# Block sums of the output matrix kept in float32 through DRAM, their additions queued behind the splits, and the last third of the last group by plain products

## The chip, the core and the metric

The kernel runs on one core of one Trainium2 chip. The time is the device time of one execution in microseconds (us). Before the change it is 1063.64 us, the median of 3 runs that lie between 1061.75 and 1066.62. TensorE multiplies matrices, VectorE, ScalarE and GpSimd (POOL in the profile) work on tiles in on-chip memory, and SyncE (SP) issues most transfers. "Granted clock" is TensorE's clock as a share of 2.4 GHz.

## The reference, cut to what matters

```
x   = attention(q, k, v, bias(w1, b1, w2))      # 2304 tokens x 512
x   = moe1(x)                                   # 2304 x 512
gate = 1 / (1 + exp(-(x @ w_gate)))             # 2304 x 1536
val  = x @ w_val                                # 2304 x 1536
out  = (gate * val) @ w_out                     # 2304 x 512, float32
```

Everything is float32. The change touches only the last three lines, the second MLP.

## The kernel before, in words

**Numbers.** TensorE multiplies float16. Each float32 matrix is therefore scaled and kept as two float16 halves, a high one (a rounded copy) and a low one (what the rounding left), and one float32 product becomes three float16 products: high by high, high by low, low by high. `w2h16[0]`, `[1]` and `[2]` are the split matrices w_gate, w_val and w_out, each as 12 row blocks of 128 by 512; `w2f[2]` is w_out still in float32, in the same memory.

**Groups.** The 2304 tokens are 18 tiles of 128, in five groups of 4, 2, 4, 4 and 4 tiles. Groups 0 and 1 are computed by plain products: `gate_val` makes one of 12 blocks of the 1536 hidden columns at a time (24 matmuls on TensorE, L1446; a sigmoid on ScalarE, L1451; the product of the two on VectorE, L1452; and the split into halves `gv`, L1315 on ScalarE and L1316 on VectorE), `second_out` multiplies by w_out (L1649). Groups 2 to 4 replace the eight products of a two-by-two block multiplication by seven, at the price of sums of blocks made beforehand: sums of weight blocks (`w2_sums`), of input blocks (`x2_sums`, `next_sums`), and of the blocks of w_out. `gate7` makes one third (`jc` 0, 1, 2) of a group's hidden columns that way (products L1410, additions on VectorE L1334 and on POOL L1225, the split of the results into pieces `ap`), and `out7` multiplies that third by w_out (L1557), adding into four result tiles `c`. The last third of the last group has its own `out_last`, which ends in the output.

**The block sums of w_out before the change.** For each `jc` four sums of four blocks are needed. `out_adds` makes them in float32 on POOL, three tiles at a time, as soon as the third of w_out is decoded. After all 12 splits of w_out, `out_split` scales each sum (ScalarE, L1249), rounds it (ScalarE, L1250), takes the low half (POOL), and stores both halves to a scratch tensor `to_d` in DRAM. Behind the plain groups `out_sums` loads the halves back: three of the four sums into a tile of their own (`w3s`), the fourth over the block b12 of `w2h16[2]`, which no later product of groups 2 to 4 reads.

**What sets the order.** The decoding of w_out, its additions, its scale, its splits (`w2_split`: the scaled copy `w2tmp` on POOL, L722, or on ScalarE, L720; the high half on ScalarE, L723; the low half on POOL, L724) and the sums' splits form a list of units, which `take` deals out between the gate blocks of group 0: 5 cost units before each of the first 8 blocks, then 7. Within an engine instructions run in the order of the code, except where `issue_after` queues something behind a named instruction: the sums of weights and of group 2's input (`fs`, `w2s`, `x2s`) stand on VectorE behind the low half of the tenth gate block, `glob["so"]`. `next_sums(3, ...)` makes the input sums of group 3, half of them per call, behind the last VectorE instruction of `gate7(0)` of group 2. Working tiles (`fr`, `c`, the eight product tiles `prod`) are rings: an instruction that writes one waits until the last reader of its previous content is done.

Of the kernel before, what the change touches and what calls it, by code (L numbers as in the profile page):

```python
# [102 lines left out]
def attn_moe_kernel(  # L103
# [20 lines left out]
    to_d = dram.tile([3, 128, 4, 2, 2, 256], F16, name="to_d")  # L124
# [1104 lines left out]
    def out_adds(jc):  # L1229
        if jc == 0:  # L1230
            four = [sw_p.tile([128, 3, 2, 256], F32, name=f"w2s{m}{n}") for n in (1, 2) for m in range(2)]
            tmps.update((n, four[n // 3][:, n % 3]) for n in range(12))
# [3 lines left out]
        padd(u, b12, b11, ALU.subtract)  # L1236
        padd(x, b22, u, ALU.subtract)
        padd(y, b22, b12, ALU.subtract)
        padd(v, b21, x, ALU.subtract)

    def behind_splits(jc):
        with tc.issue_after(glob["split"].ins):
            out_split(jc)

    def out_split(jc):
        for n in range(4):
            f = tmps[4 * jc + n]
            d = xs_p.tile([128, 2, 2, 256], F16, name=f"x2s{n}")
            act.activation(out=f, in_=f, func=ACTF.Copy, scale=sw[:, jc, S_O:S_O + 1])  # L1249
            act.activation(out=d[:, 0], in_=f, func=ACTF.Copy)  # L1250
            padd(d[:, 1], f, d[:, 0], ALU.subtract)
            sp.dma_start(out=to_d[jc, :, n], in_=d)
# [10 lines left out]
    units += [(1, lambda jc=jc: behind_splits(jc)) for jc in range(3)]  # L1263
# [21 lines left out]
    xb = {}  # L1285
# [4 lines left out]
    def load_x2(g):  # L1290
        n, o = sizes[g], first[g]
        t = ring("xb", [128, 4, 4, 2, 128], F16)
# [8 lines left out]
    grow("fr", 2, ctx, "left")  # L1301
# [208 lines left out]
    def out_sums(jc):  # L1510
        b11, b21, b12, b22 = out_blocks(jc)
        st_ = w3_p.tile([128, 3, 2, 2, 256], F16, name=f"w3s{jc}")
        sp.dma_start(out=st_, in_=to_d[jc, :, 1:4])
        for l in range(2):
            sp.dma_start(out=b12(l), in_=to_d[jc, :, 0, l])

        def part(n):
            return lambda l, kk=None: st_[:, n, l] if kk is None else st_[:, n, l, kk]
        osum[jc] = dict(b11=b11, b21=b21, b22=b22, t1=b12, t2=part(0), t3=part(1), t4=part(2))
# [9 lines left out]
    def gate7(jc, xs_):  # L1529
# [50 lines left out]
    def out_last(g, jc, ps):  # L1580
        w = osum[jc]
        a, b, c = (f32t() for _ in range(3))
        c11, c12, c21, c22 = cs[g]

        def done_(c_, p, th, e, halves=((0, 2),)):
            act.activation(out=c_, in_=c_, func=ACTF.Copy, scale=col(CO))
            for lo, hi in halves:
                dve.scalar_tensor_tensor(out=c_[:, lo:hi], in0=p[:, lo:hi], scalar=col(CO), in1=c_[:, lo:hi],
                                         op0=ALU.mult, op1=ALU.add)
                put(g, th, e, c_, range(lo, hi), (sp, act))  # L1590

        act.activation(out=a, in_=oproduct(ps["a", 1, 1], w["b11"]), func=ACTF.Copy)
        add(b, oproduct(ps["s", 2], w["t2"]), a)
        add(c11, c11, a)
        add(c, oproduct(ps["s", 3], w["t3"]), b)
        add(c22, c22, c)
        p2 = oproduct(ps["a", 1, 2], w["b21"])
        done_(c11, p2, 0, 0)
        add(c21, c21, c)
        add(c12, c12, b)  # L1600
        p5 = oproduct(ps["s", 1], w["t1"])
        add(c12, p5, c12)
        done_(c22, p5, 1, 1)
        p4 = oproduct(ps["a", 2, 2], w["t4"])
        done_(c21, p4, 1, 0)
        p3 = oproduct(ps["s", 4], w["b22"])
        done_(c12, p3, 0, 1, ((0, 1), (1, 2)))
# [84 lines left out]
    grow("fr", 6, ctx, "left")  # L1692
# [91 lines left out]
```

## Time and profile before

| | |
|---|---|
| median of 3 runs | 1063.64 us (1061.75 to 1066.62) |
| profiled execution | 1058.2 us, its span 1056.4 us |
| TensorE busy | 890.7 us, 84% |
| VectorE busy | 819.7 us, 78% |
| ScalarE busy | 681.5 us, 65% |
| POOL busy | 573.7 us, 54% |

The shares are means over stages with different limits; the stage in question runs from about 640 us to the end. A timeline row gives a start, a length, an engine, a line of the kernel, the operation, out<-in and a count; in brackets stands the idle time of the engine ahead of it and what ended that.

### The profile page before, as it was taken

To read this page: it belongs to the slowest core of one execution; us is meant where nothing else is said; L and a number is where in the kernel's file an instruction comes from. 1 tells how busy PE (TensorE), PEld (TensorE's weight loads), DVE (VectorE), ACT (ScalarE), POOL (GpSimd) and SP (SyncE) were. 2 spreads that over 40 slices of the span, in tenths; PEclk is the share of its full clock that TensorE was granted. 3 is DMA by queue.
4 is the path that set the end of the run, shared out by engine and by line. 5 is a ranking of instruction groups with operands and counts; after the bars stand their busy time and mean duration, and the time that the engine had idled before them with its cause. 6 is when DMAs were issued, how large, how long until landed. Compare 5 with 4: busy or idle time off the path is not lost. (4 is left out here: it accounts for less than half of the span.)

```text
span 1056.4 us, 25115 instructions
## 1 busy us (share of the span) xinstructions
PE 890.7 (84%) x9944; PEld 664.0 (63%) x9944; DVE 819.7 (78%) x1546; ACT 681.5 (65%) x1352; POOL 573.7 (54%) x506
## 2 busy tenths in 40 slices
PE   2646665778878899999989788887899989999997
PEld 2624444555656666776766464344478878888886
DVE  6879899876767757676758977579975997877888
ACT  4788886768877888888868986774342433443432
POOL 3357656657566665566543579347001446787355
PEclk9776576689999999999999999998989999999999
DMA  7978999899999999999678344012103131013001
GB/s 225 298 229 221 244 248 242 228 208 216 188 195 194 180 207 180 182 208 218 132 188 310 130 141 150 1 40 100 71 20 131 41 110 41 1 61 103 9 2 41
DMA packets 266838, 156.71 MB, mean 148 GB/s; under 512 B 217312, under 2 KB 239840, under 8 KB 266720
## 3 DMA queue, kind: packets, MB, share of 16 engines
q1 hardware_dynamic: 262848, 151.44, 58.9%
q0 software_dynamic: 2048, 1.58, 0.6%
q10 hardware_dynamic: 1824, 2.09, 0.5%
q8 instruction: 78, 1.28, 0.5%
q14 instruction: 40, 0.33, 0.1%
HBM read 87.17 MB, written 25.43 MB: 107 GB/s over the span
## 5 line engine op out<-in xcount | busy, mean ns | idle before, releaser
L618 POOL TENSOR_TENSOR p<-p,p 128x1024 f16<-128x1024 f32 x72 | 159.1, 2209 | 122.4 <-ACT p L617 80.7
L1225 POOL TENSOR_TENSOR ap<-fr,ap 128x512 f16<-128x512 f32 x45 | 59.1, 1327 | 141.7 <-ACT ap L1525 137.1
L606 ACT ACTIVATE p<-p,m,sc 128x576 f32<-128x576 f32 x144 | 123.9, 862 | 2.4
L1334 DVE TENSOR_TENSOR fr<-prod,fr 128x512 f32<-128x512 f32 x144 | 96.1, 686 | 35.9 <-PE prod L1410 16.3
L1446 PE MATMUL s_ps<-xb,w2f 128*128 128x512 f16 (+1 forms) x576 | 105.5, 345 | 21.8 <-DVE fr L1452 20.6
L599 DVE CUSTOM_DVE_ANT_0 p<-score,gk 128x576 f32<-128x576 f32 x144 | 103.0, 751 | 12.2 <-PE score L581 7.8
L848 PE MATMUL x2ps<-lt,w1f 128*128 128x128 f16 x1728 | 105.0, 220 | 3.2 <-ACT lt L836 2.0
L848 PEld LDWEIGHTS <-w1f 128*128 128x128 f16 x1728 | 100.2, 99 | 3.5 <-issue 1.1
L1446 PEld LDWEIGHTS <-w2f 128*128 128x128 f16 x576 | 59.2, 103 | 68.2 <-issue 28.9
L642 PE MATMUL xps<-gk,pt 128*128 128x64 f16 (+1 forms) x2240 | 87.3, 202 | 14.5 <-DMA pt<-p 12.5
L642 PEld LDWEIGHTS <-pt 128*128 128x128 f16 (+1 forms) x2240 | 82.0, 107 | 24.2 <-DMA pt<-p 14.7
L1410 PEld LDWEIGHTS <-w2f 128*128 128x128 f16 x864 | 84.5, 98 | 14.2 <-issue 4.3
L465 PEld LDWEIGHTS <-mask 128*128 128x128 f16 (+1 forms) x1312 | 59.6, 115 | 52.4 <-issue 23.8
L1525 ACT ACTIVATE ap<-fr 128x512 f16<-128x512 f32 x63 | 38.8, 628 | 79.9 <-DVE fr L1536 44.0
L1557 PEld LDWEIGHTS <-ap 128*128 128x128 f16 x756 | 73.8, 98 | 10.1 <-DVE c L1334 1.5
L791 PE MATMUL hps<-w1f,xt 128*128 128x512 f16 x312 | 75.8, 389 | 5.0 <-DVE gk L264 2.3
L576 PE MATMUL score<-gk,qt 64*128 64x512 f16 x384 | 61.2, 426 | 14.4 <-DVE m L599 6.3
L465 PE MATMUL bp<-rhs,mask 128*128 128x64 f16 (+1 forms) x960 | 47.9, 216 | 27.5 <-DVE gb L491 10.6
L1410 PEld LDWEIGHTS <-w2s 128*128 128x128 f16 x648 | 63.4, 98 | 8.7 <-issue 1.4
L791 PEld LDWEIGHTS <-xt 128*128 128x128 f16 x384 | 37.5, 101 | 47.1 <-issue 11.8
L617 ACT ACTIVATE p<-p 128x1152 f16<-128x1152 f32 x54 | 62.4, 1157 | 6.1 <-DMA pt<-p 4.1
L604 ACT ACTIVATE m<-m,sc 128x1 f32<-128x1 f32 x144 | 39.3, 286 | 36.2 <-DVE m L599 35.9
(236 smaller groups left out, 2164.8 us busy)
## 6 DMA issues: line engine op xcount, KB each, us to landing
gk<-bias_d SPq DMA_DIRECT2D x24, 576.0 KB
wraw<-in_moe_w_out_dram SPq DMA_DIRECT2D x20, 512.0 KB
sraw<-in_q_dram SPq DMA_DIRECT2D x12, 384.0 KB
sraw<-in_k_dram SPq DMA_DIRECT2D x12, 384.0 KB
sraw<-in_v_dram SPq DMA_DIRECT2D x12, 384.0 KB
bias_d<-gk SPq DMA_DIRECT2D x8, 576.0 KB
qraw<-in_q_dram SPq DMA_DIRECT2D x64, 64.0 KB
kv<-in_k_dram SPq DMA_DIRECT2D x32, 128.0 KB
```

The source lines that it names most:

```text
L465: pe.matmul(big[0:np_, jj // 8, o:o + 64], lhsT, rhs[i].rearrange("p c h g -> p (c h g)"), start=(i == 0), stop=(i == 1),)
L599: dve.tensor_tensor_reduce(out=pp[:, hh], in0=score[:, 960 * hh:960 * hh + S], in1=bi, scale=1.0, scalar=-3.0e38, op0=ALU.add, op1=ALU.max ...
L606: act.activation(out=pp[:, hh], in_=pp[:, hh], func=ACTF.Exp, bias=m[:, 2 + hh:3 + hh], scale=col(C), accum_out=sm[:, c + hh:c + hh + 1])
L617: act.activation(out=hi, in_=pp, func=ACTF.Copy)
L618: pool.tensor_tensor(out=p16[:, :, 640:1152], in0=view(pp, 0, [[640, 2], [1, 512]]), in1=view(p16, 0, [[1280, 2], [1, 512]]), op=ALU.subtract)
L642: pe.matmul(o, a, b_, start=(n == 0), stop=(n == len(seq) - 1))
L791: pe.matmul(h, xt[:, xl, kk, off:off + 128], win16[:, 2 * kk + n, wl], start=(kk == 0 and xl == 0 and wl == 0), stop=(kk == 3 and xl == 1),)
L848: pe.matmul(ps[:, dc], wout16[:, f, wl, 128 * dc:128 * dc + 128], lt[:, ll, f], start=(n == 0), stop=(n == 23))
L1334: glob["dve"] = dve.tensor_tensor(out=out_, in0=a, in1=b, op=op)
L1410: pe.matmul(p[:, jf, 0:nn], w(wl, kk, jf), x(xl, kk), start=(m == 0), stop=(m == 5))
L1446: pe.matmul(ps[:, 0:n], w[:, 4 * (j // 4) + c, wl, o:o + 128], xx[:, 0:n, c, xl, :], start=(m == 0), stop=(m == 11))
L1557: pe.matmul(p[:, tt], a[:, al, kk, 128 * tt:128 * tt + 128], w(wl, kk), start=(m == 0), stop=(m == 5))
```

## The change: what it does

1. `out_adds` no longer stands where w_out is decoded: its twelve additions and stores are queued behind the last split, for `jc` 0 and 1 on POOL, for `jc` 2 on VectorE (`dadd`). The float32 sums go to `to_d` as they are. `out_split` is gone.
2. `out_sums` loads each float32 sum into one of the four `c` tiles (float32, unused until then), scales and rounds it on ScalarE and takes the low half on VectorE. There are twelve such loads, of 256 KB each.
3. Before it is overwritten, block b12 of the last third is saved to DRAM (`b12_d`), and it is loaded back behind group 3. The last third of the last group then multiplies by the plain blocks: `gate7` returns only the four gate pieces, and `out_last` makes four result blocks of 24 products each.
4. The first half of `next_sums(3, ...)` stands ahead of group 2's products. The `fr` ring has three tiles instead of two up to the plain groups' end, five instead of six behind it; the input tile of a group is as long as the group.

```diff
-    to_d = dram.tile([3, 128, 4, 2, 2, 256], F16, name="to_d")
+    to_d = dram.tile([3, 128, 4, 2, 256], F32, name="to_d")
+    b12_d = dram.tile([128, 2, 2, 256], F16, name="b12_d")
...
     def out_adds(jc):
+        with tc.issue_after(glob["split"].ins):
+            out_adds_(jc, padd if jc < 2 else dadd)
+
+    def dadd(out_, a, b, op=ALU.add):
+        dve.tensor_tensor(out=out_, in0=a, in1=b, op=op)
...
-        padd(u, b12, b11, ALU.subtract)
...
-            act.activation(out=f, in_=f, func=ACTF.Copy, scale=sw[:, jc, S_O:S_O + 1])
-            act.activation(out=d[:, 0], in_=f, func=ACTF.Copy)
-            padd(d[:, 1], f, d[:, 0], ALU.subtract)
-            sp.dma_start(out=to_d[jc, :, n], in_=d)
+        plus(u, b12, b11, ALU.subtract)
...
+        for n, f in enumerate((u, x, y, v)):
+            sp.dma_start(out=to_d[jc, :, n], in_=f)
...
-    units += [(1, lambda jc=jc: behind_splits(jc)) for jc in range(3)]
+    units += [(1, lambda: sp.dma_start(out=b12_d, in_=w2h16[2][:, 8:10, :, 256:512]))]
...
-    grow("fr", 2, ctx, "left")
+    grow("fr", 3, ctx, "left")
...
-        sp.dma_start(out=st_, in_=to_d[jc, :, 1:4])
-        for l in range(2):
-            sp.dma_start(out=b12(l), in_=to_d[jc, :, 0, l])
...
+        s_ = sw[:, jc, S_O:S_O + 1]
+        for n in (1, 2, 3, 0):
+            f, d = ctile(n), part(n - 1) if n else b12
+            sp.dma_start(out=f, in_=to_d[jc, :, n])
+            act.activation(out=d(0), in_=f, func=ACTF.Copy, scale=s_)
+            dve.scalar_tensor_tensor(out=d(1), in0=f, scalar=s_, in1=d(0), op0=ALU.mult, op1=ALU.subtract)
...
-            if (fh, th) != (0, 1):
+            if plain_ or (fh, th) != (0, 1):
                 ps["a", th + 1, fh + 1] = piece(y, padd)
+        if plain_:
+            return ps
...
-    grow("fr", 6, ctx, "left")
+    grow("fr", 5, ctx, "left")
...
+    next_sums(3, 0, add)
     for g in range(2, 5):
         p0 = gate7(0, xs_)
         if g == 2:
             with tc.issue_after(glob["dve"].ins):
-                for t in range(2):
-                    next_sums(3, t, add)
+                next_sums(3, 1, add)
...
-        p2 = gate7(2, xs_)
+        p2 = gate7(2, xs_, g == 4)
...
+        if g == 3:
+            sp.dma_start(out=w2h16[2][:, 8:10, :, 256:512], in_=b12_d)
```

`out_last` now reads, per result block, `p += a[th, kh] @ blk[kh, e]` over both `kh`, both row blocks and the three pairs of halves, and one scaled addition on VectorE per block (two for the last) before the store.

How the order on the engines moves, in three places. **First place:** ScalarE right behind the scale of w_out, before (`w2s` are the block sums, `x2s` their halves, `gv` a gate block's high half, `fr<-s_ps` a sigmoid, L720 and L723 the split of w_out):

```order
L1451 ACTIVATE fr<-s_ps,sw 128x512
L1315 ACTIVATE gv<-fr 128x512
L1451 ACTIVATE fr<-s_ps,sw 128x512
L720 ACTIVATE w2tmp<-w2f_9698,sw 128x512 x2
L1249 ACTIVATE w2s_10750<-w2s_10750,sw 128x512 x3
L1249 ACTIVATE w2s_10751<-w2s_10751,sw 128x512 x3
L1249 ACTIVATE w2s_10752<-w2s_10752,sw 128x512 x3
L1249 ACTIVATE w2s_10753<-w2s_10753,sw 128x512 x3
L723 ACTIVATE w2f_9698<-w2tmp 128x512 x2
L1250 ACTIVATE x2s_11022<-w2s_10750 128x512
```

and in the changed kernel:

```order
L1448 ACTIVATE fr<-s_ps,sw 128x512
L1312 ACTIVATE gv<-fr 128x512
L721 ACTIVATE w2tmp<-w2f_9699,sw 128x512 x2
L724 ACTIVATE w2f_9699<-w2tmp 128x512 x2
L1448 ACTIVATE fr<-s_ps,sw 128x512
L721 ACTIVATE w2tmp<-w2f_9699,sw 128x512 x2
L724 ACTIVATE w2f_9699<-w2tmp 128x512
L1312 ACTIVATE gv<-fr 128x512
L724 ACTIVATE w2f_9699<-w2tmp 128x512
```

The twelve scalings and the copies into `x2s` are no longer in the queue; gate copies and sigmoids follow the splits directly.

**Second place:** ScalarE at the third and fourth gate block (counted from 0: sigmoids two and three), before (`x2ps` is the end of the first MLP, `wraw` and `w2f` the decoding of w_out, L1178 the sum of squares for its scale):

```order
L193 ACTIVATE w2f_9698<-wraw 128x1024
L194 ACTIVATE wraw<-wraw 128x1024
L723 ACTIVATE w2f_9696<-w2tmp 128x512
L723 ACTIVATE w2f_9697<-w2tmp 128x512
L853 ACTIVATE x_10687<-x2ps 128x4x128
L1451 ACTIVATE fr<-s_ps,sw 128x512
L193 ACTIVATE w2f_9698<-wraw 128x1024
L194 ACTIVATE wraw<-wraw 128x1024
L856 DMA x_d<-x_10687 128x1024
L723 ACTIVATE w2f_9697<-w2tmp 128x512
L1451 ACTIVATE fr<-s_ps,sw 128x512
```

and in the changed kernel, where the lines stand one to three further:

```order
L724 ACTIVATE w2f_9698<-w2tmp 128x512 x2
L1179 ACTIVATE w2junk,w2st<-w2f_9699 128x1024
L194 ACTIVATE w2f_9699<-wraw 128x1024
L195 ACTIVATE wraw<-wraw 128x1024
L724 ACTIVATE w2f_9698<-w2tmp 128x512
L1179 ACTIVATE w2junk,w2st<-w2f_9699 128x1024
L854 ACTIVATE x_10688<-x2ps 128x4x128
L1448 ACTIVATE fr<-s_ps,sw 128x512 x2
L194 ACTIVATE w2f_9699<-wraw 128x1024
L195 ACTIVATE wraw<-wraw 128x1024
```

Both sigmoids now stand together, behind two sums of squares, a further decoding pair and the copy of `x`; before, one stood ahead of a decoding pair and the other behind it.

**Third place:** SP's queue where the sums are loaded back, before (`out_dram<-ob` are output stores of group 1, `xx<-x_d` loads of group 3's input):

```order
L1658 DMA out_dram<-ob 128x512 x3
L1515 DMA w2f_9698<-to_d 128x2x256 x4
L1513 DMA w3s_12099<-to_d 128x3072
L1513 DMA w3s_12103<-to_d 128x3072
L1513 DMA w3s_12107<-to_d 128x3072
L1461 DMA xx<-x_d 128x1024 x2
L1515 DMA w2f_9698<-to_d 128x2x256 x2
L1662 DMA out_dram<-ob 64x512 x2
L1658 DMA out_dram<-ob 128x512
L1471 DMA xt_d<-xx 128x2048
```

and in the changed kernel:

```order
L1516 DMA c_12066<-to_d 128x512
L1516 DMA c_12083<-to_d 128x512
L1458 DMA xx<-x_d 128x1024 x2
L1516 DMA c_12071<-to_d 128x512
L1516 DMA c_12075<-to_d 128x512
L1516 DMA c_12079<-to_d 128x512
L1516 DMA c_12100<-to_d 128x512
L1516 DMA c_12088<-to_d 128x512
L1516 DMA c_12092<-to_d 128x512
L1659 DMA out_dram<-ob 64x512 x2
L1655 DMA out_dram<-ob 128x512
L1516 DMA c_12096<-to_d 128x512
```

Seven of the twelve loads now stand behind the first pair of group 3's input loads, the last of them behind three output stores too; before, only two halves for b12 did.

## Rows read from the trace of the kernel before

**Rows 1.** Page: busy tenths in 40 slices of 26.4 us

```profile
PE   2646665778878899999989788887899989999997
...
DVE  6879899876767757676758977579975997877888
```

**Rows 2.** Stretches: window, length, busy (instructions) of PE, PEld, DVE, ACT, POOL, clock, DMA

```profile
690.80:718.40 27.60, 23.34 (x136) 12.99 (x134) 26.18 (x30) 19.77 (x35) 13.67 (x11) 1.00 0.11 39
718.40:742.10 23.70, 18.34 (x98) 10.31 (x96) 23.70 (x24) 9.27 (x20) 18.43 (x12) 0.86 0.35 134
742.10:780.00 37.90, 34.82 (x211) 21.83 (x210) 37.87 (x68) 14.65 (x28) 0.00 (x0) 0.91 0.13 42
867.00:1031.10 164.10, 163.12 (x1494) 145.73 (x1492) 131.93 (x170) 62.69 (x106) 104.85 (x92) 1.00 0.11 39
```

**Rows 3.** Waits of PE, 636 to 1057 us: total us, times, longest us

```profile
PE s_ps L1446 <- DVE fr L1452: 20.6, 7, 5.4
PE prod L1410 <- DVE fr L1334: 3.9, 2, 2.7
```

**Rows 4.** Timeline of POOL, PE and ACT, 645 to 666 us: start, length first

```profile
645.56 4.73 POOL L1225 TENSOR_TENSOR w2s<-w2f 128x512 f32<-128x512 f32 x3
...
645.84 5.35 PE L1446 MATMUL s_ps<-xb,w2f 128*128 128x512 f16 x24 [0.62 <-DVE fr L1452]
...
651.96 0.63 ACT L723 ACTIVATE w2f<-w2tmp 128x512 f16<-128x512 f32 x1 [4.32 <-POOL w2tmp L722]
...
653.58 1.12 ACT L193 ACTIVATE w2f<-wraw 128x1024 f32<-128x1024 f32 x1
...
655.02 7.03 PE L1446 MATMUL s_ps<-xb,w2f 128*128 128x512 f16 x24 [3.83 <-DVE fr L1452]
...
665.53 10.43 PE L1446 MATMUL s_ps<-xb,w2f 128*128 128x512 f16 x40 [3.48 <-DVE fr L1452]
```

**Rows 5.** Timeline of ACT and DVE, 678 to 692 us

```profile
679.67 7.44 ACT L1249 ACTIVATE w2s<-w2s,sw 128x512 f32<-128x512 f32 x12
...
690.78 0.69 DVE L1316 TENSOR_TENSOR gv<-fr,gv 128x512 f16<-128x512 f32 x1 [11.51 <-ACT gv L1315]
```

**Rows 6.** Groups of DVE by form, 718.4 to 742.1 us: busy us, mean ns

```profile
L1334 DVE TENSOR_TENSOR fs<-xb 128x512 f32<-128x512 f16 x4 | 6.4, 1639 | 0.0
...
L1334 DVE TENSOR_TENSOR fs<-fs,xb 128x512 f32<-128x512 f32 x1 | 0.7, 679 | 0.0
```

**Rows 7.** Groups of DVE by form, 745.5 to 780 us

```profile
L1334 DVE TENSOR_TENSOR fs<-w2f 128x512 f32<-128x512 f16 x13 | 8.5, 688 | 0.0
...
L1316 DVE TENSOR_TENSOR gv<-fr,gv 128x256 f16<-128x256 f32 x4 | 1.7, 425 | 0.0
```

**Rows 8.** Timeline of PE, 725 to 783 us: gate blocks of group 1

```profile
725.87 4.93 PE L1446 MATMUL s_ps<-xb,w2f 128*128 128x256 f16 x24 [5.36 <-DVE fr L1452]
...
765.46 8.22 PE L1446 MATMUL s_ps<-xb,w2f 128*128 128x256 f16 x48 [3.08 <-DVE fr L1452]
...
776.75 5.40 PE L1446 MATMUL s_ps<-xb,w2f 128*128 128x256 f16 x48
```

**Rows 9.** Groups of PE by form, 688 to 796 us: last the idle time before

```profile
L1446 PE MATMUL s_ps<-xb,w2f 128*128 128x256 f16 x288 | 37.7, 296 | 12.7 <-DVE fr L1452 12.7
```

**Rows 10.** Timeline of PE and DVE at group 2's first product

```profile
796.30 1.47 PE L1410 MATMUL prod<-xb,w2f 128*128 128x256 f16 x12 [1.14 <-ACT ob L1653]
...
799.19 0.69 DVE L1334 TENSOR_TENSOR fr<-prod,fr 128x512 f32<-128x512 f32 x1 [7.70 <-PE prod L1410]
```

**Rows 11.** Timeline of SP and DVE, 836 to 843 us

```profile
836.56 0.80 SPq L1461 DMA_DIRECT2D xx<-x_d  x2
...
840.08 2.04 DVE L1334 TENSOR_TENSOR ts<-xx 128x256 f32<-128x256 f16 x3
```

**Rows 12.** Timeline of PE and DVE at the end

```profile
1048.12 1.47 PE L1557 MATMUL prod<-w2f,ap 128*128 128x256 f16 x12
...
1050.98 2.18 DVE L1588 SCALAR_TENSOR_TENSOR c<-prod,sc,c 128x512 f32<-128x512 f32 x4
```

More of the change, by code (lines that the diff above doesn't have):

```diff
@@ L1229, in out_adds, with out_adds_ @@
     def out_adds(jc):
+        with tc.issue_after(glob["split"].ins):
+            out_adds_(jc, padd if jc < 2 else dadd)
+    def dadd(out_, a, b, op=ALU.add):
+        dve.tensor_tensor(out=out_, in0=a, in1=b, op=op)
+    def out_adds_(jc, plus):
         if jc == 0:
@@ L1235, in out_adds @@
         u, x, y, v = (tmps[4 * jc + n] for n in range(4))
-        padd(u, b12, b11, ALU.subtract)
[L1237 to L1248, printed above, removed]
-            act.activation(out=f, in_=f, func=ACTF.Copy, scale=sw[:, jc, S_O:S_O + 1])
-            act.activation(out=d[:, 0], in_=f, func=ACTF.Copy)
-            padd(d[:, 1], f, d[:, 0], ALU.subtract)
-            sp.dma_start(out=to_d[jc, :, n], in_=d)
+        plus(u, b12, b11, ALU.subtract)
+        plus(x, b22, u, ALU.subtract)
+        plus(y, b22, b12, ALU.subtract)
+        plus(v, b21, x, ALU.subtract)
+        for n, f in enumerate((u, x, y, v)):
+            sp.dma_start(out=to_d[jc, :, n], in_=f)
     steps = [(m, jc) for jc in range(3) for m in range(2)]
@@ L1291, in load_x2 @@
         n, o = sizes[g], first[g]
-        t = ring("xb", [128, 4, 4, 2, 128], F16)
+        t = ring("xb", [128, n, 4, 2, 128], F16)
         sp.dma_start(out=t[:, 0:n], in_=x2_d[o:o + n].rearrange("t p c l q -> p t c l q"))
@@ L1527, in piece, with gate7 @@
         return p
-    def gate7(jc, xs_):
+    def gate7(jc, xs_, plain_=False):
         gates, ps = {}, {}
@@ L1580, in out_last @@
     def out_last(g, jc, ps):
[L1581 to L1585, printed above, removed]
+        blk = dict(zip(((0, 0), (1, 0), (0, 1), (1, 1)), out_blocks(jc)))
+        for c_ in cs[g]:
             act.activation(out=c_, in_=c_, func=ACTF.Copy, scale=col(CO))
[L1587 to L1607, printed above, removed]
+        for n, (th, e) in enumerate(((0, 0), (0, 1), (1, 1), (1, 0))):
+            c_ = cs[g][2 * th + e]
+            p = ps_b.tile([128, 2, 256], F32, name="prod", tag="prod")
+            for tt in range(2):
+                m = 0
+                for kh in range(2):
+                    a = ps["a", th + 1, kh + 1]
+                    for kk in range(2):
+                        for (al, wl) in ((0, 0), (0, 1), (1, 0)):
+                            pe.matmul(p[:, tt], a[:, al, kk, 128 * tt:128 * tt + 128], blk[kh, e](wl, kk),
+                                      start=(m == 0), stop=(m == 11))
+                            m += 1
+                if n == 3:
+                    dve.scalar_tensor_tensor(out=c_[:, tt], in0=p[:, tt], scalar=col(CO), in1=c_[:, tt],
+                                             op0=ALU.mult, op1=ALU.add)
+                    put(g, th, e, c_, (tt,), (sp, act))
+            if n < 3:
+                dve.scalar_tensor_tensor(out=c_, in0=p, scalar=col(CO), in1=c_, op0=ALU.mult, op1=ALU.add)
+                put(g, th, e, c_, range(2), (sp, act))
     def out7(g, jc, ps):
```

## The prediction

> **What bounds the kernel now.** I read the slices of the page first [rows 1]: in the two slices from 713 to 766 us VectorE stands at 9 while TensorE is at 7 and 8, and from about 770 us on TensorE is at 9 in all slices but two. Then the table of stretches [rows 2]: from 690.8 to 780 VectorE is busy 87.8 of 89.2 us and TensorE 76.5; from 867 to 1031 it is the other way round (TensorE 163.1 of 164.1). So the first stretch ends when VectorE is through its sums, the second when TensorE is through its products, and time taken off VectorE in the second buys nothing. The waits of TensorE say the same [rows 3]: 20.6 us in seven waits for VectorE's L1452, the second step of the gate, which stands in VectorE's queue among the sums; then only 3.9 us in two waits for L1334, both near 850 us.
>
> **Part 1: additions queued behind the splits (640 to 702 us).** Before, the first three of the twelve additions (POOL, 4.73 us) stand between two scalings of the splits; ScalarE waits 4.32 us for such a scaling, the sigmoid of the fourth gate block stands right behind it, at 652.6, and TensorE starts its sixth block only at 655.02 after 3.83 us of waiting [rows 4]. That wait's cause goes, and four of the twelve additions move to VectorE. But the order of the changed kernel also puts two sigmoids behind a scaled pair, two copies and a sum of squares that stood elsewhere (the second place shown in the change). Worked through with the durations of rows 4: POOL's scaling can come at about 645.6 instead of 650.3 (where the three additions end), so ScalarE's copy behind it ends near 647.5; then one more copy (0.63), a square and a decoding pair (each 1024 columns, 1.12 an instruction), a copy, a square and a copy of x2 (0.63, 1.12 and 0.6, the last by the copy's length) stand ahead, with about 1 us of waiting for POOL between them, so the third block is emptied near 655 instead of about 644 (8 us before the fourth's 652.6) and TensorE's fifth block starts near 656 instead of 645.84. Against that, the next wait (3.48 us, at 665.5) goes. I then get TensorE through its twelfth block near 699.5 instead of 702.5, with six products of the second matrix done instead of eighteen, which is 2.6 us of work at 0.22 each (5.35 us for 24 in rows 4): the two cancel. I take 0, bounds 6 us better (all waits of this stretch go, 20.6 - 12.7 = 7.9 by rows 3 and 9) and 6 us worse (the late emptying is not caught up).
>
> **Part 2: the splits of the block sums leave the stage (679 to 796 us).** Removed from ScalarE: twelve scalings (7.44 us) and twelve copies; VectorE waits 11.51 us for a gate copy behind the scalings and the first four copies [rows 5]. Removed from POOL: twelve low halves, 18.4 us of its time in 718.4 to 742.1 [rows 2]. VectorE pays for them: beside POOL a 512-column addition takes 1639 ns, and the last of that view, which already runs beside an idle POOL, 679 [rows 6]; later, with POOL idle, 688 and for 256 columns 425 [rows 7]. The stretch holds 24 instructions [rows 2]; their forms in that view (eleven, of which rows 6 has the first and the last) sum to 26.6 us, as two of them reach over its ends; at the durations of rows 7 (19 of 0.69, 5 of 0.42) they are 15.2. So VectorE gets some 11 us back there.
> The Trainium skill speaks against counting this (Perfetto Trace Analysis, Optimizing Scalar/DVE Operations): since VectorE and POOL share a read port, moving work between the two might not help. By that rule of the Trainium skill the 11 us would be spent again, because the twelve low halves return as VectorE instructions, and the part would be worth nothing more than the earlier start.
> By the rows the twelve low halves return on VectorE at 12 x 0.69 = 8.3 us, but only four of them (2.8 us) stand ahead of the last gate of the stage; the other eight, and fourteen instructions of the next group's sums, stand between the last gate and the first product, where VectorE waited 7.7 us for TensorE [rows 10].
> The sums can also start earlier: they stand behind the tenth block's gate in both kernels, which by part 1 is emptied near 692 instead of 695.9. Together VectorE gains 4 + 11 - 3 = 12 us up to its last gate. What TensorE can gain: its waits in 688 to 796, 12.7 us [rows 9], and what runs at the lower clock after a wait (granted 0.86 and 0.91 of 2.4 GHz over the stretches from 718 and from 742 [rows 2], so for part of them at 1.2): 24 products in 4.93 us at 725.87 and 48 in 8.22 at 765.46, where 48 take 5.40 at full clock [rows 8], so 2.2 + 2.8 = 5.0. That is 17.7 us. From 699.5, TensorE's remaining work (210 products of 0.22 and 288 of 0.1125, which is 5.40 by 48: 78.6 us) would end at 778 without any wait; before it ended at 795.2. Bounds: 18 if VectorE is never late; 8 if it is late at two of the four places, and the load of the third group's input, which now stands behind thirteen stores in SP's queue, holds the sums up by up to 3 us. VectorE's 12 us are enough for all but the last few waits: I take **-15**.
>
> **Part 3: the sums come back as float32 (around the first product).** Twelve loads of 256 KB pass through four tiles, so three rounds; each round is an issue (0.4), the landing, a scaled copy on ScalarE (0.63) and a subtraction (0.69). The nearest row for the landing: two such loads are issued at 836.56 and VectorE reads them at 840.08, 3.5 us at most [rows 11]. A round is thus at most 5 us. The first is early (its loads stand behind the fourth output store, 20 us ahead of need). The second starts behind the subtractions next to the last gate, some 8 us ahead of the first product, the third 3 us later than the second ends; its last load stands in SP's queue behind three output stores that wait for the last output copy. That gives the last subtraction at 6 us after the first product's start. VectorE's first addition on a product stands behind eleven of the twelve, so it comes at about 5 us instead of 2.9 [rows 10] (799.19, the first product at 796.30). Products have eight tiles of 12 products, 12 x 0.11 = 1.3 us each, so TensorE runs 10.5 us before it must wait: cost 0. Bounds: 0 to +4, the latter if a landing takes 5 us.
> The next group's sums for one of its two tiles now stand ahead of the first product, so half of the 28 instructions that crowd VectorE around 840 leave, and with them most of the 3.9 us of waits [rows 3]: **-2.5**, bounds 0 and -3.9. The reload of the b12 block behind group 3 has 70 us until it is read: 0.
>
> **Part 4: the last third by plain products.** 96 products instead of 84: 12 x 0.11 = +1.3 us on TensorE, which runs here without a wait. Removed: seven blocks' additions, so behind the last product only one addition of half a block is left. Before, the last product ends at 1049.59 and VectorE at 1053.16 [rows 12], 3.6 us; four pieces took 2.18, so one and its wait are about 0.7. Together 1.3 - 2.9 = **-1.6**, bounds 0 and -2.5.
>
> **Sum.** 0 - 15 + 0 - 2.5 - 1.6 = -19.1. The profiled execution took 1058.2 us, so 1039.1 by its own time. It stood 5.4 us below the median of the runs shown (1063.64); at that median the sum gives **1044.5**. Bounds of the terms added: -30 and +12.
>
> **Rivals.**
> Partial: the late sigmoids of part 1 cost their 6 us and are not caught up, and VectorE is late at half of its places (-8 in part 2): 6 - 8 - 2.5 - 1.6 = -6.1, 1057.5. For it: the order does put the sigmoids there, and VectorE was the bound. Against: TensorE waited in that stretch already [rows 4].
> VectorE and POOL come out even: the 11 us are no gain, because what comes back to VectorE (twelve subtractions and four additions, 16 x 0.69 = 11 us) is paid ahead of the gates. The earlier start (-4) and the tail (-1.6) stay: -5.6, 1058.0. For it: every instruction that leaves POOL does reappear. Against: eight of the twelve stand behind the last gate. It is also what the rule quoted in part 2 from the Trainium skill (Perfetto Trace Analysis) would make of the change.
> The four tiles hold up the products (the slower side): the queues of VectorE and ScalarE are in order, and the subtractions stand ahead of the additions that empty product tiles. It decides from the point at which the last subtraction comes later than 10.5 us after the first product's start. If a round takes 22 us instead of 5 (SP held behind a store that waits for ScalarE, and ScalarE at a copy that waits for a load), the last subtraction comes at -8 + 44 = 36 us, and TensorE loses 25.5 us against the gain of 19.1: +6.4, 1070. For it: SP's queue does hold these loads behind such stores. Against: rows 11, at 3.5 us.
>
> **Chances.** The forecast (part 2 between 10 and 18 us) 0.62; partial 0.14; even 0.14; four tiles 0.10. A measurement here tells about 0.5%, 5.3 us, from no change, so faster means below 1058.3. The forecast lies there as a whole; partial and even are centred just below that bound, so 0.16 of their 0.28 count as faster and 0.12 as the same; of four tiles 0.07 count as slower and 0.03 as the same. Faster 0.78, same 0.15, slower 0.07. The range that leaves out 2 in 10 goes from 1034 (parts 1 and 2 some 5 us each better than taken) to 1060, across the two middle rivals.
>
> **What would show it.** Part 1: no addition between POOL's scalings; the fifth gate block's start on TensorE, 656 by me. Part 2: no ScalarE work on block sums behind the scale; additions on input and weight sums at 0.69, not 1.64, after POOL's twelve splits; TensorE's waits for the gate below 5 us in all after the twelfth block; first product near 781. Part 3: VectorE's first addition on a product 5 us behind it; the waits near 850 below 1.5 us. Part 4: the last addition within 1 us of the last product. The forecast is wrong if the first product starts later than 790, or if TensorE waits among the first twenty products.

## The result and the profile after

| | changed | before | ratio, 95% interval |
|---|---|---|---|
| first comparison | 1049.45 us (1047.28 to 1050.26, 4 runs) | 1063.16 us | 0.9863 [0.9835, 0.9891] |
| second comparison (after_again) | 1044.98 us (1043.19 to 1048.64, 6 runs) | 1065.65 us | 0.9818 [0.9789, 0.9846] |

The changed kernel is faster: 1049.45 us against a forecast of 1044.5, inside the range. In the first comparison 13.7 of the forecast 19.1 us came, in the second 20.7. The traces say why two comparisons of one kernel differ: the time up to the last transposition of attention's output, where every engine runs the same instructions in the same order in both kernels, is not the same from run to run. That transposition (L691 before, L692 after) and the first product of group 2 stand on TensorE at, before, in two executions (the shown one and before_again):

```profile
551.82 0.66 PE L691 MATMUL xtp<-id_sb,xn 128*128 128x128 f32 x4 [3.19 <-DVE xn L678]
```

```profile
561.39 0.66 PE L691 MATMUL xtp<-id_sb,xn 128*128 128x128 f32 x4 [3.26 <-DVE xn L678]
...
803.95 1.47 PE L1410 MATMUL prod<-xb,w2f 128*128 128x256 f16 x12 [1.14 <-ACT ob L1653]
```

and after, in the first comparison and in after_again:

```profile
562.00 0.66 PE L692 MATMUL xtp<-id_sb,xn 128*128 128x128 f32 x4 [3.24 <-DVE xn L679]
...
793.02 1.47 PE L1407 MATMUL prod<-xb,w2f 128*128 128x256 f16 x12 [2.34 <-ACT ob L1650]
```

```profile
555.02 0.66 PE L692 MATMUL xtp<-id_sb,xn 128*128 128x128 f32 x4 [3.07 <-DVE xn L679]
...
785.54 2.67 PE L1407 MATMUL prod<-xb,w2f 128*128 128x256 f16 x12 [2.64 <-DMA c<-to_d]
788.01 1.98 PE L1407 MATMUL prod<-x2s,w2s 128*128 128x256 f16 x12
```

So I read every trace from that point, P (the start of the transposition). From P to the first product, and from there to the end of the span:

| kernel | P at | P to first product | first product to end | P to end |
|---|---|---|---|---|
| before, 3 executions | 551.8, 561.4, 560.3 | 244.5, 242.6, 243.1 | 260.1, 260.1, 260.1 | 504.6, 502.6, 503.1 |
| changed, 2 executions | 562.0, 555.0 | 231.0, 230.5 | 255.5, 257.2 | 486.5, 487.7 |

Means: 503.4 to 487.1, or 16.3 us; 12.6 of them ahead of the first product (forecast 15), 3.8 behind it (forecast 4.1). The forecast, set from P of the shown execution, was 229.2 us to the first product (781 less 551.8). Behind the first product the two executions of the changed kernel differ by TensorE's clock: in after_again, after a wait of 2.64 us, the first two products took 2.67 and 1.98 us instead of 1.47 each, 1.7 us more (granted clock 0.61 from 785.54 to 789.90 us, for most of it the lower level of 1.2 GHz); in the first comparison, after 2.34 us, it was 1.00.

What was read before has these answers. TensorE's waits from the fifth gate block to the end (us in total, times, longest), beside [rows 3]:

```profile
PE s_ps L1443 <- DVE fr L1449: 10.7, 1, 10.7
PE prod L1407 <- ACT ob L1650: 2.3, 1, 2.3
PE prod L1407 <- ACT fr L1612: 1.1, 1, 1.1
PE prod L1595 <- DVE c L1599: 0.6, 1, 0.6
PE prod L1407 <- DVE c L1331: 0.2, 1, 0.2
```

Seven waits for the gate have become one, at the fifth block, and none is left behind it. TensorE's timeline there, and VectorE's costliest groups from 705 to 790 us (busy us, mean ns), beside [rows 4, 6]:

```profile
669.39 11.81 PE L1443 MATMUL s_ps<-xb,w2f 128*128 128x512 f16 x47 [10.72 <-DVE fr L1449]
...
708.58 5.34 PE L1443 MATMUL s_ps<-xb,w2f 128*128 128x512 f16 x24
```

```profile
L1331 DVE TENSOR_TENSOR fs<-w2f 128x512 f32<-128x512 f16 x24 | 15.6, 682 | 0.0
L1331 DVE TENSOR_TENSOR fs<-fs,w2f 128x512 f32<-128x512 f32 x18 | 12.3, 681 | 0.0
...
L1331 DVE TENSOR_TENSOR fs<-xb 128x512 f32<-128x512 f16 x4 | 2.6, 680 | 0.0
```

The same four additions on `xb` took 1639 ns each before. The stretches, beside [rows 2] (window, length, busy of PE, PEld, DVE, ACT, POOL, clock):

```profile
669.40:705.00 35.60, 35.60 (x160) 16.04 (x160) 18.94 (x36) 25.81 (x44) 16.93 (x14) 0.96 0.21 74
705.00:793.00 88.00, 85.69 (x540) 52.66 (x539) 79.49 (x144) 38.99 (x73) 0.00 (x0) 1.00 0.20 62
```

VectorE at the first product (793.02), beside [rows 10]: its first addition, and the last subtraction on a returned sum:

```profile
796.80 0.68 DVE L1331 TENSOR_TENSOR fr<-prod,fr 128x512 f32<-128x512 f32 x1
...
798.18 0.75 DVE L1518 SCALAR_TENSOR_TENSOR w3s<-c,sw,w3s 128x512 f16<-128x512 f32 x1 [0.36 <-ACT w3s L1517]
```

From the fifth block on TensorE is the bound: idle for the 2.3 us ahead of the first product only, at full clock from 705 us. At the end, beside [rows 12]:

```profile
1043.54 1.47 PE L1595 MATMUL prod<-w2f,ap 128*128 128x256 f16 x12 [0.65 <-DVE c L1599]
1045.05 0.48 DVE L1599 SCALAR_TENSOR_TENSOR c<-prod,sc,c 128x256 f32<-128x256 f32 x1 [1.56 <-PE prod L1595]
```

VectorE ends 0.5 us behind the last product instead of 3.6. Two things in the account of the change are to be put more sharply. The split that the additions are queued behind is the last of w_val, not of w_out: POOL's eight run from 659.35 to 672.11 us, ahead of w_out's splits. And in the kernel before only POOL's low halves of the sums stood behind the splits of w_out: ScalarE's twelve scalings ran from 679.67 us on [rows 5], ahead of all but two of w_out's scaled copies.

### The profile page after: what moved, and what is told of

The parts are those of the page before. It is cut to its first block, busy times and chain, and to the rows that moved or that the text cites. A ratio compares the mean times of both kernels' runs of the same rounds, so it can differ in the third digit from the quotient of the medians.

```text
span 1048.5 us, 25126 instructions
## 1 busy us (share of the span) xinstructions
PE 886.8 (85%) x9952; PEld 666.1 (64%) x9956; DVE 796.4 (76%) x1551; ACT 673.8 (64%) x1336; POOL 540.9 (52%) x487
## 5 line engine op out<-in xcount | busy, mean ns | idle before, releaser
L600 DVE CUSTOM_DVE_ANT_0 p<-score,gk 128x576 f32<-128x576 f32 x144 | 102.9, 750 | 16.0 <-PE score L582 10.7
L1443 PE MATMUL s_ps<-xb,w2f 128*128 128x512 f16 (+1 forms) x576 | 101.0, 333 | 14.2 <-DVE fr L1449 10.7
L466 PEld LDWEIGHTS <-mask 128*128 128x128 f16 (+1 forms) x1312 | 62.4, 118 | 56.6 <-issue 25.0
L1407 PEld LDWEIGHTS <-w2f 128*128 128x128 f16 x864 | 84.5, 98 | 13.9 <-issue 4.1
L1443 PEld LDWEIGHTS <-w2f 128*128 128x128 f16 x576 | 57.0, 100 | 55.7 <-issue 16.5
L792 PE MATMUL hps<-w1f,xt 128*128 128x512 f16 x312 | 79.8, 403 | 5.3 <-DVE gk L265 2.5
L1559 PEld LDWEIGHTS <-ap 128*128 128x128 f16 x672 | 65.6, 98 | 8.1 <-DVE c L1331 0.5
```

The costliest lines, as they stand in the source:

```text
L466: pe.matmul(big[0:np_, jj // 8, o:o + 64], lhsT, rhs[i].rearrange("p c h g -> p (c h g)"), start=(i == 0), stop=(i == 1),)
L600: dve.tensor_tensor_reduce(out=pp[:, hh], in0=score[:, 960 * hh:960 * hh + S], in1=bi, scale=1.0, scalar=-3.0e38, op0=ALU.add, op1=ALU.max ...
L792: pe.matmul(h, xt[:, xl, kk, off:off + 128], win16[:, 2 * kk + n, wl], start=(kk == 0 and xl == 0 and wl == 0), stop=(kk == 3 and xl == 1),)
L1407: pe.matmul(p[:, jf, 0:nn], w(wl, kk, jf), x(xl, kk), start=(m == 0), stop=(m == 5))
L1443: pe.matmul(ps[:, 0:n], w[:, 4 * (j // 4) + c, wl, o:o + 128], xx[:, 0:n, c, xl, :], start=(m == 0), stop=(m == 11))
L1559: pe.matmul(p[:, tt], a[:, al, kk, 128 * tt:128 * tt + 128], w(wl, kk), start=(m == 0), stop=(m == 5))
```

## Experiments

All differences are read from P unless a ratio stands beside them. Repeats of one kernel lie within 2 us to the first product and 1.7 behind it, so a single execution shows no less. After_again is the changed kernel's second execution, whose runs stand beside those of the second comparison.

**The third gate tile.** In the changed kernel's order ScalarE has the third and fourth sigmoids late. Reduced to two gate tiles, the order is the old one there; with the third tile alone in the kernel before, it is the new one. So what I had put down to the additions in part 1 is the tile's doing, and two kernels test what it costs. The first has two gate tiles in the changed kernel:

```diff
-    grow("fr", 3, ctx, "left")
+    grow("fr", 2, ctx, "left")
...
-    grow("fr", 5, ctx, "left")
+    grow("fr", 6, ctx, "left")
```

> The changed kernel with two gate tiles (fr) instead of three up to the end of the plain groups, and six instead of five behind it. The order on ScalarE then has the third and fourth sigmoids where the kernel before has them. Theory A (the third tile, not the additions, put both sigmoids late): TensorE's 10.7 us wait ahead of the fifth gate block goes, the fifth block starts about 94 us behind the last transposition of attention instead of 107, and the total is 5 to 10 us below the changed kernel's 1049, so 1039 to 1044. Rival B (the third tile is what took away the 12.7 us of waits between 690 and 790): the early wait goes, but waits for the gate of 5 to 12 us come back behind the splits, and the total is 1049 to 1056. Rival C (my prediction's reading: the late sigmoids come from the moved additions): the wait ahead of the fifth block stays at 8 us or more, total 1049.

Measured: 1045.25 us, ratio to before 0.983 [0.9808, 0.9851]; 229.5 us to the first product (changed: 230.8), 486.0 to the end (487.1). TensorE's timeline:

```profile
659.41 5.34 PE L1443 MATMUL s_ps<-xb,w2f 128*128 128x512 f16 x24 [1.19 <-DVE fr L1449]
671.02 10.33 PE L1443 MATMUL s_ps<-xb,w2f 128*128 128x512 f16 x41 [6.28 <-DVE fr L1449]
...
694.06 10.52 PE L1443 MATMUL s_ps<-xb,w2f 128*128 128x512 f16 x48
...
709.06 2.78 PE L1443 MATMUL s_ps<-xb,w2f 128*128 128x256 f16 x24 [0.81 <-DVE fr L1449]
712.66 2.78 PE L1443 MATMUL s_ps<-xb,w2f 128*128 128x256 f16 x24 [0.83 <-DVE fr L1449]
...
766.68 2.78 PE L1443 MATMUL s_ps<-xb,w2f 128*128 128x256 f16 x24 [0.29 <-DVE fr L1449]
```

The 10.7 us wait goes, as theory A had it, and five waits of 9.4 us in all stand in its place, 7.5 of them ahead of the splits' end: neither A's gain nor B's loss. The total of 1045.25 came near A's 1039 to 1044 for another reason, the early P (557.9).

The tile alone in the kernel before, with the input tile and the later ring shortened to make room:

```diff
-    grow("fr", 2, ctx, "left")
+    grow("fr", 3, ctx, "left")
...
-        t = ring("xb", [128, 4, 4, 2, 128], F16)
+        t = ring("xb", [128, n, 4, 2, 128], F16)
...
-    grow("fr", 6, ctx, "left")
+    grow("fr", 5, ctx, "left")
```

> The kernel before with only the third gate tile (three up to the end of the plain groups, five behind) and the shorter input tile that makes room for it. Theory A: the wait ahead of the fifth gate block appears (8 to 12 us), the three waits of 0.6, 3.8 and 3.5 us around it go, and the total is 0 to 6 us above the kernel before: 1063 to 1069. Rival B: the third tile also takes away half or more of the 12.7 us of waits behind 690 us; total 1053 to 1060. Rival C: no wait of over 5 us ahead of the fifth block; 1063.

Measured: 1062.84 us, 0.9992 [0.9974, 1.0011]. TensorE waits for the gate in three waits of 18.1 us in all, the longest 10.7, where before_again has nine waits of 21.5; behind the twelfth block they are 7.3 us against 13.5, so the tile gives back there what it costs at the fifth. To the first product 241.5 us, against 243.4: 1.9 less, no more than repeats differ by, and the whole time, 1.0 below the kernel before, does not show it (A had 0 to 6 above). Rival C is out: the late sigmoids come with the tile, without any addition moved.

**The additions.** Back where they were, all on POOL:

```diff
-        with tc.issue_after(glob["split"].ins):
-            out_adds_(jc, padd if jc < 2 else dadd)
+        out_adds_(jc, padd)
```

> The changed kernel with the twelve additions where they were, all on POOL, between the scalings of the splits. My prediction put their move at 0 (6 either way): 1049, between 1046 and 1052. Rival: with the additions back, ScalarE's copies wait 4 us and more for POOL's scalings again and TensorE waits for the gate among blocks five to eight: 1052 to 1058. In both the 10.7 us wait ahead of the fifth block stays if the third gate tile causes it; if the moved additions cause it, it falls below 4 us and the total to 1040 to 1045.

Measured: 1050.25 us, 0.9876 [0.985, 0.9903]. 231.4 us to the first product (230.8), 489.6 to the end (487.1); the 10.7 us wait stays. Moving the additions is worth 0.6 us up to the first product, which is under what one execution tells. The rest of the 2.5 stands behind it, where no addition was moved, and there it is the clock again (granted 0.57 from 790.26 to 797.10 us, behind a wait of 3.63):

```profile
790.26 2.72 PE L1406 MATMUL prod<-xb,w2f 128*128 128x256 f16 x12 [3.63 <-ACT ob L1649]
792.77 2.77 PE L1406 MATMUL prod<-x2s,w2s 128*128 128x256 f16 x12
795.33 1.86 PE L1406 MATMUL prod<-xb,w2f 128*128 128x256 f16 x12
```

At 1.47 us each these three products would take 2.9 us less, and the stretch behind the first product would be 255.4 instead of 258.3 us, that of the first execution of the changed kernel (255.5).

**The splits of the sums.** Kept ahead of the stores, with the halves loaded back:

```diff
-        for n, f in enumerate((u, x, y, v)):
-            sp.dma_start(out=to_d[jc, :, n], in_=f)
+    def out_split(jc):
+        for n in range(4):
+            f = tmps[4 * jc + n]
+            d = xs_p.tile([128, 2, 2, 256], F16, name=f"x2s{n}")
+            act.activation(out=f, in_=f, func=ACTF.Copy, scale=sw[:, jc, S_O:S_O + 1])
+            act.activation(out=d[:, 0], in_=f, func=ACTF.Copy)
+            padd(d[:, 1], f, d[:, 0], ALU.subtract)
+            sp.dma_start(out=to_d[jc, :, n], in_=d)
...
```

> The changed kernel with the sums split ahead of the stores, as before (twelve scalings and twelve copies on ScalarE, twelve low halves on POOL, halves loaded back); the additions stay behind the splits, the plain last third and the moved input sums stay. My prediction: this part is worth 15 us (8 to 18), so 1061 to 1064, with VectorE's additions at 1.3 to 1.6 us again beside POOL and waits of TensorE for the gate of 10 us or more. Rival (VectorE and POOL come out even, because the twelve low halves return on VectorE): 1049 to 1053.

Measured: 1056.27 us, 0.9934 [0.9912, 0.9955], between the two totals expected; 241.45 us to the first product:

```profile
561.16 0.66 PE L692 MATMUL xtp<-id_sb,xn 128*128 128x128 f32 x4 [3.10 <-DVE xn L679]
...
802.61 1.47 PE L1419 MATMUL prod<-xb,w2f 128*128 128x256 f16 x12 [1.14 <-ACT ob L1659]
```

Against the changed kernel's 230.8 the splits' move is worth 10.7 us: within my bounds of 8 to 18, well under 15, and far from the rival's 0. VectorE's additions beside POOL are back at 1.64 us (two in 3.20 us at 736.69). Behind the twelfth block TensorE waits 7.6 us for the gate, in three waits, less than the 10 expected; the 10.7 us at the fifth block come on top of them, as in the changed kernel. Against the third tile alone (241.5) the run also shows the moved additions at 0.1 us, that is, at nothing that can be told.

Which engine's share? Twelve subtractions on POOL alone were put back:

```diff
+    def lows(jc):
+        with tc.issue_after(glob["split"].ins):
+            for n in range(4):
+                d = xs_p.tile([128, 2, 2, 256], F16, name=f"x2s{n}")
+                padd(d[:, 1], tmps[4 * jc + n], w2h16[2][:, 4 * jc:4 * jc + 2, 0, 0:256], ALU.subtract)
...
+    units += [(1, lambda jc=jc: lows(jc)) for jc in range(3)]
```

> The changed kernel with twelve subtractions of 512 columns added on POOL behind the splits of w_out (results unused, nothing is stored of them), where the low halves of the sums were. It brings back POOL's share of the removed work without ScalarE's scalings and copies. Theory P (VectorE beside POOL is what made the stretch long): VectorE's additions take 1.2 to 1.6 us for some 18 us, TensorE waits 5 to 10 us for the gate, and the first product comes 5 to 10 us later; total 5 to 10 us above the changed kernel of this call. Rival S (ScalarE's scalings and copies, which the gate copies stood behind, were the cost): VectorE's additions lengthen, but TensorE's waits stay below 2 us and the time within 2 us.

Measured: 1055.53 us, 0.9917 [0.9889, 0.9945], 10.6 us above after_again; 239.1 us to the first product, 8.3 later, of which some 7 stand behind the twelfth block, where the added work is (86.4 us from its end to the first product, against 79.1 and 79.4). POOL's timeline, and VectorE's groups from 698 to 718 us:

```profile
696.37 1.16 POOL L725 TENSOR_TENSOR w2f<-w2tmp,w2f 128x512 f16<-128x512 f32 x1 [0.69 <-ACT w2f L724]
...
700.41 18.36 POOL L1226 TENSOR_TENSOR x2s<-w2s,w2f 128x512 f16<-128x512 f32 x12
```

```profile
L1338 DVE TENSOR_TENSOR fs<-w2f 128x512 f32<-128x512 f16 x7 | 11.1, 1623 | 0.0
...
L1320 DVE TENSOR_TENSOR gv<-fr,gv 128x512 f16<-128x512 f32 x2 | 1.4, 692 | 2.4 <-ACT gv L1319 2.4
```

and TensorE's timeline in that time:

```profile
713.73 4.45 PE L1450 MATMUL s_ps<-xb,w2f 128*128 128x256 f16 x24 [2.33 <-DVE fr L1456]
...
722.38 2.78 PE L1450 MATMUL s_ps<-xb,w2f 128*128 128x256 f16 x24 [2.48 <-DVE fr L1456]
```

Twelve instructions whose results nothing reads slow VectorE's additions from 0.68 to 1.62 us, and TensorE waits for the gate again, 4.8 us in two waits (5 to 10 expected): theory P. VectorE waits for no POOL instruction there, so it is not a tile held by the added work. (The Trainium skill, Perfetto Trace Analysis, Optimizing Scalar/DVE Operations, says that VectorE and POOL share a read port, and the slower additions agree with that. Its inference that moving work between the two might not help does not hold here, where the work comes back at a time at which POOL is idle: the stretch to the first product became 10.7 us shorter.)

ScalarE's share, put back alone (against the edit above):

```diff
-                padd(d[:, 1], tmps[4 * jc + n], w2h16[2][:, 4 * jc:4 * jc + 2, 0, 0:256], ALU.subtract)
+                for l in (1, 0):
+                    act.activation(out=d[:, l], in_=tmps[4 * jc + n], func=ACTF.Copy, scale=sw[:, jc, S_O:S_O + 1])
```

> The changed kernel with twenty-four scaled copies of 512 columns added on ScalarE behind the splits of w_out (results unused), where its twelve scalings and twelve copies of the sums were, and nothing on POOL. With the added POOL work the first product came 8.3 us later behind the last transposition of attention, with all of the removed work 10.6. Theory P (POOL's share is the larger): 1 to 4 us above the changed kernel of this call's scale (1045 to 1049), the first product 1 to 4 us later than 230.8 us behind that point. Rival (ScalarE's queue costs as much as POOL's): first product 6 us later or more.

Measured: 1050.95 us, 0.9878 [0.9848, 0.9907]; 234.9 us to the first product, 4.1 later, at the edge of the 1 to 4 expected. So putting back POOL's share costs twice what ScalarE's does; the two add to 12.4, more than the 10.7 of all together. But ScalarE's share also works through POOL. The added copies hold up the splits of w_out, whose low halves POOL then makes until 716.48 us, 160.5 behind P, instead of 704.30, 142.3 behind P, in the changed kernel. There they fall beside VectorE's sums, which take 1.6 us each again:

```profile
702.61 4.35 POOL L725 TENSOR_TENSOR w2f<-w2tmp,w2f 128x512 f16<-128x512 f32 x3 [1.01 <-ACT w2f L724]
...
702.74 4.77 DVE L1339 TENSOR_TENSOR fs<-w2f 128x512 f32<-128x512 f16 x3
```

In the changed kernel the sums begin at 705.88 us, when POOL is through. What ScalarE's queue costs by itself these runs do not show.

**Four tiles for the returning sums.** Two instead:

```diff
-            f, d = ctile(n), part(n - 1) if n else b12
+            f, d = ctile(n % 2), part(n - 1) if n else b12
```

> The changed kernel with the twelve float32 sums coming back through two tiles instead of four, so six rounds instead of three. My prediction took a round at 5 us at most and the four tiles' cost at 0 (0 to 4): here the last subtraction comes 10 to 15 us later, behind the point from which TensorE has no free product tile, and the time is 2 to 8 us above the changed kernel. The rival of the four tiles (a round of 22 us): 40 us and more above it. If the rounds are hidden anyway: within 1 us.

Measured: 1051.78 us, 0.9877 [0.9853, 0.9901]. The first product is not later (229.5), but 261.7 us lie behind it instead of 256.3: 5.4 more. The last subtraction on a returned sum starts 20.1 us behind the first product (806.91 against 786.84) instead of 5.2, 14.9 later. TensorE's timeline, some 32 us behind the first product:

```profile
818.79 2.72 PE L1407 MATMUL prod<-x2s,w2s 128*128 128x256 f16 x12 [2.98 <-ACT fr L1415]
823.30 1.47 PE L1407 MATMUL prod<-xb,w2f 128*128 128x256 f16 x12 [1.79 <-DVE fr L1331]
```

The mechanism of the slower rival exists, at a size that fits rounds of about 5 us, and four tiles keep it off.

**The moved half of the input sums.** Back behind the first seven products:

```diff
-    next_sums(3, 0, add)
     for g in range(2, 5):
...
-                next_sums(3, 1, add)
+                for t in range(2):
+                    next_sums(3, t, add)
```

> The changed kernel with both halves of the third group's input sums behind the first seven products, as before. My prediction: 2.5 us (0 to 3.9) above the changed kernel of this call, with 3 to 4 us of TensorE's waits for VectorE about 50 us behind the first product. Rival: the half that now stands ahead of the first product delays the first additions there, so without it the first product's additions come earlier and the time is the same or up to 1 us lower.

Measured: 1050.65 us, 0.9869 [0.9837, 0.9901]; 259.8 us behind the first product instead of 256.3, so the move is worth 3.4 (4.3 against the execution of the changed kernel whose first products run at full clock, as they do here). The total is 5.7 us above after_again, where at most 3.9 were expected; 2.5 of it lie ahead of P (557.5 against 555.0). TensorE's waits 50 us behind the first product:

```profile
838.38 1.47 PE L1407 MATMUL prod<-xb,w2f 128*128 128x256 f16 x12 [1.97 <-ACT fr L1612]
842.02 1.48 PE L1407 MATMUL prod<-x2s,w2s 128*128 128x256 f16 x12 [2.17 <-DVE c L1331]
...
846.66 1.47 PE L1407 MATMUL prod<-xb,w2s 128*128 128x256 f16 x12 [0.53 <-DVE fr L1331]
```

**The plain last third**, undone (the old `out_last`, no saved block):

```diff
-        p2 = gate7(2, xs_, g == 4)
+        p2 = gate7(2, xs_)
...
-            sp.dma_start(out=w2h16[2][:, 8:10, :, 256:512], in_=b12_d)
...
```

> The changed kernel with the last third of the last group by seven products, as before, without the saved block b12. My prediction put that part at 1.6 us (0 to 2.5): 1 to 2.5 us above the changed kernel of this call, and the stretch from the last product to the end 2 to 3 us longer. Rival (12 more products on TensorE eat it): no difference, within 0.5 us.

Measured: 1049.14 us, 0.9851 [0.9819, 0.9883], 4.2 us above after_again; but its P stands at 560.6, that of after_again at 555.0. 256.4 us behind the first product, against 255.5 and 257.2. TensorE's and VectorE's last rows:

```profile
1039.32 1.47 PE L1558 MATMUL prod<-w2f,ap 128*128 128x256 f16 x12
```

```profile
1041.59 2.18 DVE L1589 SCALAR_TENSOR_TENSOR c<-prod,sc,c 128x512 f32<-128x512 f32 x4
```

VectorE ends 3.0 us behind the last product (1043.77 against 1040.79), so 2.5 us of tail go with the plain third, as I had it; 1.3 us of products and a wait of 0.65 come in. What is left, some 0.6 us, is under what these runs can tell; the 1 to 2.5 us expected are not shown.

**The kernel before, again,** for its trace.

> The kernel before, for its trace alone. Its shown execution had 551.8 us up to the last transposition of attention and 504.6 behind it, at 1058.2 us in all, 5 us below the median. Theory V (the first part varies between runs, the second does not): 555 to 561 us in the first part and 503.5 to 505.5 in the second. Rival W (the kernel before is short in the first part, 552, and the changed one long): 551 to 553, with 508 and more in the second.

> The kernel before once more, for its trace alone, with the same two expectations as for before_again: by theory V another first part than there by 2 us or more, and the second part within 1 us of 504.6.

Measured: 1065.8 and 1065.21 us, with P at 561.4 and 560.3 and 502.6 and 503.1 us behind it. The second part is steady within 2 us, but lies 2.0 and 1.5 us below 504.6, outside both bands I had given for it, as the P of 561.4 lies 0.4 above its band. P differed by 1.1 us between them, not by the 2 I had asked for. After_again had been expected at 1045 to 1047 us with P at 557 to 559 by theory V, at 1049 to 1050 with P at 561 to 562 by W (there: the third tile lengthens the part ahead of P); it took 1044.98, with P at 555.0. Over all fourteen executions P lay between 551.8 and 562.0 (the kernel before 551.8 to 561.4, the changed one 555.0 to 562.0), and the part behind it does not follow it: theory V, not W. At most it gives a little back: in both kernels the execution with the earliest P has the longest part behind it, by 1.2 to 2.0 us. What moves P stays open; its spread begins early (the first score product at 68.6 us in the shown execution of before, at 72.7 in the first of after).

## Why the prediction was right, and where its sizes were off

| step | forecast | measured from P |
|---|---|---|
| part 1, additions queued behind a split | 0 | 0.1 to 0.6 us better, not told apart from 0 |
| the third gate tile | not priced | 1.9 us better in the kernel before, 1.3 worse in the changed one, each under 2 |
| part 2, splits leave the stage | -15 | -10.7 |
| part 3, sums back through four tiles | 0 | first product's wait 2.3 to 2.6 instead of 1.1 us: +1.2 to +1.5, inside the -10.7; in one of two executions 1.7 more behind it, at the lower clock |
| part 3, half of the input sums moved | -2.5 | -3.4 |
| part 4, plain last third | -1.6 | about -0.6 by the rows of the tail; not told apart from 0 |
| together, P to end | -19.1 | -16.3 |

The mechanism was the forecast one: VectorE's sums beside POOL's low halves were the bound from 690 to 780 us, the low halves went, VectorE's additions fell from 1639 to 682 ns, TensorE's waits for the gate behind the twelfth block went to nothing and its clock to 1.00 (705 to 793 us). The rival by which VectorE and POOL come out even is refuted by halves_kept and pool_lows; the partial rival's late sigmoids exist, but are caught up. In the order third tile, additions, splits, the stretch from P to the first product goes from 243.4 to 241.5, 241.45 and 230.8 us: the edits that were tested account for all of the 12.6.

The step that was mis-sized is part 2, "I take -15": the splits alone measure 10.7, and up to the first product the whole change brought 12.6. Part of it was in part 1. I had the fifth block start 104.2 us behind P (656) and the twelfth end 147.7 behind it (699.5) with six products of the second matrix done. Measured they stand at 107.4 and 151.9, also with six: the late sigmoids cost 4 us more than I took, some 1.5 of them because the 47 products behind the long wait took 11.81 us, where 0.22 each would make 10.3. ring2 shows that this is the tile: its twelfth block ends at 704.58, 146.7 us behind P, with four products done. I had seen the late sigmoids in the order and worked out a price for them, but put them into the wrong edit, and the edit that causes them I had not priced at all. From the twelfth block to the first product I forecast 81.5 us (699.5 to 781) and measured 79.1 (713.92, where the block of 708.58 ends, to 793.02): there is no wait for the gate left, so what the tile costs early it returns here, and its sum is small (ring2, with two tiles, takes 82.8 us for this stretch).

The kernel before had about 1 us less to lose than I thought: the shown execution has 244.5 us to the first product, two others 242.6 and 243.1.

One sum of the prediction is wrong: the bounds of its terms add up to -30 and +2 (6 - 8 + 4), not +12. Neither the forecast nor the range was taken from it.

What I named as signs: additions at 0.68 us (0.69 said); no gate wait behind the twelfth block (under 5 us said); VectorE's first addition on a product 3.8 us behind it (5 said; 796.80 against 793.02); the waits 50 us behind the first product 1.3 us (under 1.5 said); the last addition 0.5 us behind the last product (1 said); and TensorE does not wait among the first twenty products. One sign failed as written: the first product was to start before 790 and started at 793.02. By P, which I had not used, it is 782.8 on the scale of the shown execution.

The total: the forecast was set at the median of before by adding 5.4 us to a profiled execution. That step was sound, since those 5 us lie ahead of P; but the same spread is in the changed kernel's runs, so one comparison of 4 runs gives 13.7 us and the next 20.7, around the 16.3 that the steady part shows. That the second total lies within half a microsecond of the forecast is luck: its traced execution has an early P, 555.0. No run beats the changed kernel beyond its interval; the one with two gate tiles equals it.

## What to carry to other kernels

When VectorE's queue sets the pace, look at what POOL does in the same stretch: twelve POOL instructions whose results nothing reads cost 8.3 us here, and the same work done later on VectorE, beside an idle POOL, cost 1.2 to 3.2 us at the first product. Work on a third engine counts too when it moves POOL's work beside VectorE's: twenty-four copies on ScalarE cost 4.1 us that way or by their own queue. Price every edit of a diff, the buffer counts first: a third tile alone moved the third sigmoid from 92.0 to 101.1 us behind P. Compare traces from a point behind the part that the change does not touch; a spread of 10 us ahead of it is larger than most of the steps one wants to see.

## What the runs showed of the hardware that was not expected

VectorE's 512-column additions take 0.68 us alone and 1.62 to 1.64 beside POOL's subtractions, and POOL pays too: its subtraction of the same size took 1.16 us in the splits (the row at 696.37) and 1.53 (18.36 by 12) beside VectorE's additions. In pool_lows the two take turns: from 702 to 719 us eleven additions stand against eleven of POOL's subtractions. VectorE's gate step, which multiplies the sigmoid by TensorE's result `s_ps`, did not pay; it took 0.68 us in the middle of them:

```profile
702.05 4.77 DVE L1338 TENSOR_TENSOR fs<-w2f 128x512 f32<-128x512 f16 x3
...
713.00 0.68 DVE L1456 SCALAR_TENSOR_TENSOR fr<-s_ps,fr 128x512 f32<-128x512 f32 x1
```

Between the start and P the same instructions in the same order took between 551.8 and 562.0 us.
